# An FNet and GeGLU kernel: who issues two DRAM copies, and when one sum of x is formed

## The chip, the cores and the metric

The kernel runs on one core of a Trainium2 chip. A core has five engines with instruction queues of their own: TensorE (PE, with its weight loads shown as PEld), VectorE (DVE), ScalarE (ACT), GpSimd (POOL) and SyncE (SP). Sixteen DMA engines move the data for all of them. SP, ACT and POOL can each issue transfers; the profile counts those of SP as queue q1, those of ACT as q10 and those of POOL as q0. The metric is the device time in microseconds of one execution, as the median of several runs.

## What is computed

The input x has 2048 rows of 448 columns. Its rows are normalized to xn, and two results are formed from it:

```python
a = einsum("bsd,ed->bse", xn, dft_hid_re)        # 448 x 448
b = einsum("bsd,ed->bse", xn, dft_hid_im)
s = einsum("ts,bse->bte", dft_seq_re, a) - einsum("ts,bse->bte", dft_seq_im, b)   # 2048 x 2048
g = silu((gelu(xn @ w_gate) * (xn @ w_up)) @ w_down)      # 448 -> 1792 -> 448
out = x + s * g
```

Everything is float32. The kernel splits most operands into a rounded high part (the PE's fast 32-bit format) and the remainder, and multiplies high by high, high by low and low by high.

## The kernel before, in words

**The stages.** After a start of some 70 us (loads, norms, transposes, the first two feature blocks done plainly) comes the feed-forward stage: 24 *blocks*, two runs (p = 0 and 1) over features f = 2 to 13 in units of 128, each for half of the rows. Then comes the hidden transform (L988 and on), and then the long sequence transform with the matrices Cr and Ci (L1175 and on).

**One block** is the function `strassen` (L414). It forms gate and up projections of two row quarters with fewer products than the plain way: from sums of weights (s1 to s4) and sums of x (t1 to t4, and for the last columns tq). The order of the work on every engine is the order in which the Python code calls it (`manual_schedule`, L507). On PE, a block is five products x1 to x4 and x6 in five PSUM banks, with six matmuls of an earlier group's down projection (`down_one`, L372, reached by `send`) in four places of the block. The banks are the same in each block: x1 is bank 0, so the next block's first product x1 may not start before ScalarE has read this block's x1 for the gelu at L461.

On ScalarE, a block runs: a copy of x1 (L432), the high part of the late half's result (L499), the high part of the plain weights (L291), the high parts of the weight sums (L295, L296), in some blocks those of the down weights (L316) and of a sum of x (L711), the gelu of x1 (L461), the high part of the result (L477), and the second gelu (L493). VectorE subtracts the high parts and adds up the products; L299 and L300 are the low parts of the weight sums, L474, L475 and L490 handle the products.

**The weights' loop.** Each block prepares the next one's weights. SP loads the raw weights of the block after next as soon as the low parts are formed and the raw buffer is free (`load_s`, two transfers, L262 with 512 KB and L263 with 128 KB, issued behind L300). POOL forms the weight sums in the raw buffer (`sums_s`, L278 to L282) when both have landed. Then ScalarE (L295) and VectorE (L299, L300) split them, and the next load follows. So block b issues the load whose sums POOL forms in block b + 1, and which PE uses in block b + 2.

**Where the calls stand.** `strassen` gets three lists of steps: `preps[0]` runs behind x2, `preps[1]` behind the first half of x4, and `preps[2]` behind the gelu L461. It gets four steps `dn`, the down products, the last of which stands at the block's end, and two steps `late`, the unfinished end of the block before: `late[0]` stands behind x1 and `late[1]` behind x2.

**Sums in DRAM.** While these blocks run, the sums of Cr and Ci that the last stage needs are formed in DRAM, since only transfers are needed for it. For each pair j of output blocks (0 to 7), `sum_step` (L775) issues two copies of 896 KB each from the input `ca` to `sums[j]` (d = 0, in block n = 3j) and later two accumulating transfers of the same size onto them (d = 2, in block 3j + 2; for j = 0 one each in blocks 1 and 2). The copies are issued by SP (L788), ahead of the block's own steps, the accumulating ones by POOL (L790). As SP and POOL run ahead of PE, the copies of block 3j are issued right behind the weights' load of block 3j - 1, and the accumulating transfers of block 3j + 2 right behind POOL's weight sums in block 3j + 1. An accumulating transfer waits until its copy has landed.

**Sums of x for the second run.** Those are formed during the first run and in the first block of the second one, one step at a time. A step (`t_step`, L697) has three parts: the sum on VectorE (L701 to L706), its high part on ScalarE (L711), and its low part on VectorE (L715), which also issues the loads of the next step (`t_load`, L688: L691 and L695). The last two steps are `t1_steps[6]` and `t1_steps[7]`. In the first block of the second run (n = 12) the code at L897 to L901 puts the rest of step 6 into `preps`, the sum of step 7 into `preps[2]`, its high part into `dn[2]` and its low part into `dn[3]`. The first use of step 7 is in the next block, the third product (x3, L445).

Of the kernel before, what the change touches and what calls it, by code (L numbers as in the profile page):

```python
# [47 lines left out]
def fnet_geglu(ctx: ExitStack, tc: tile.TileContext, x, ca, ct, cp, et, wgu, wss, wd, out):  # L48
# [15 lines left out]
    nc = tc.nc  # L64
# [27 lines left out]
    def part(t, off, a, b):  # L92
        v = t[:, off : off + a * b].rearrange("p (a b) -> p a b", a=a)
        return v
# [209 lines left out]
    def load_d(grp):  # L304
        rv = a_r[:, 17 * P : 17 * P + 2 * D].rearrange("p (f d) -> p f d", f=2)
        nc.sync.dma_start(
            rv, wd[grp[0] * P : (grp[0] + 2) * P, :].rearrange("(f p) d -> p f d", p=P)
        )
        return rv
# [197 lines left out]
    with tc.manual_schedule():  # L507
# [180 lines left out]
        def t_load(i, p, k1, k2):  # L688
            c, e = 2 * p, 2 * p + 1
            for n, v in ({0: (e, k1), 1: (c, k1)}, {0: (e, k2)}, {1: (c, k2)}, {0: (e, k1)}, {})[i].items():  # L690
                nc.sync.dma_start(tmp(n), xw_at(*v))  # L691
            if i == 3:
                rows = [slice(0, P)] if k1 < 3 else [slice(0, 64), slice(64, P)]
                for r in rows:
                    nc.sync.dma_start(tmp(1)[r], xw_at(e, k2)[: r.stop - r.start])  # L695

        def t_step(i, places, p, k1, k2):  # L697

            a, b = tmp(0), tmp(1)

            def sub():  # L701
                if i == 1:
                    n = P if k1 < 3 else 64
                    nc.vector.tensor_sub(a[:n], a[:n], b[:n])
                else:
                    nc.vector.tensor_sub(b, *((a, b), None, (b, a), (b, a))[i])  # L706

            v = a if i == 1 else b

            def high():  # L710
                nc.scalar.activation(places()[T[i]][0], v, AF.Copy)  # L711

            def low():
                h, l = places()[T[i]]
                nc.vector.tensor_sub(l, v, h)  # L715
                t_load(i + 1, p, k1, k2)

            return sub, high, low
# [50 lines left out]
        late = (h1, l1)  # L769
# [5 lines left out]
        def sum_step(at):  # L775


            j, d = divmod(at, 3)
            halves = [slice(0, NS // 2), slice(NS // 2, NS)]
            if d == 1:  # L780
                halves = halves[:1] if j == 0 else []
            elif d == 2 and j == 0:
                halves = halves[1:]
            for n in halves if j < NK // 2 else []:
                a, b = sums[j][:, n], ca[j, min(d, 1), :, n]
                a, b = [v.rearrange("p k c -> p (k c)") for v in (a, b)]
                if d == 0:
                    nc.sync.dma_start(a, b)  # L788
                else:
                    nc.gpsimd.dma_start(a, b, accum_op=ALU.add)  # L790

# [14 lines left out]
        t1_steps = [t_step(i, t1_places, 1, 0, 1) for i in range(4)]  # L806
# [14 lines left out]
        def then(*steps):  # L821
            return lambda: [v() for v in steps]
# [7 lines left out]
        def weights(n):  # L830

            if n == len(blocks):
                return [], [], []
            slot = slots[2 if n == len(blocks) - 1 else n % 2]
            w_of[blocks[n]] = parts_of(slot)
            plain, high, low = split_s(slot)
            next_ = [lambda: load_s(blocks[n + 1][1])] if n + 1 < len(blocks) else []
            return [plain, lambda: sums_s(nc.gpsimd)], [high], [low, *next_]

        def weights_d(g):  # L840
            w_d[g], low_of[g] = prep_d(GROUPS[g], d_raw[0])
# [3 lines left out]
        def e_load(b):  # L845
            e_raw[b] = (a_r[:, : 2 * D], tmp01, tmp01, a_r[:, 2 * D : 4 * D])[b]
            nc.sync.dma_start(e_raw[b], et[b].rearrange("p r d -> p (r d)"))
# [3 lines left out]
        def e_split(b):  # L851

            r = e_raw[b]
            if b == 3:
                e_at[b] = []
                for i in range(2):
                    h, q = a_ws[:, 3584 + i * D :][:, :D], r[:, i * D : (i + 1) * D]
                    nc.scalar.activation(h, q, AF.Copy)
                    nc.vector.tensor_sub(h[64:], q[64:], h[64:].bitcast(F32))
                    e_at[b].append(h)  # L860
                return
            v = (a_ws[:, 1792:3584], a_d[1], a_ws[:, :1792])[b]
            split(v[:, : 2 * D], v[:, 2 * D :], r)
            e_at[b] = [v[:, i * D : (i + 1) * D] for i in range(4)]

        for n, (p, f) in enumerate(blocks):
            g = f // 2
            dn, q = [send] * 4, tq[p]
            prep = weights(n + 1)
            step = []  # L870
            if f % 2 == 0 and n:
                d_raw[0] = load_d(GROUPS[g])
            sum_step(n)
            if f % 2 and 1 < n < len(blocks) - 1 or n == len(blocks) - 2:
                prep[1].append(lambda: weights_d(g))
                prep[2].append(lambda: low_of[g]())
            if p == 0:
                if f == 2:
                    dn = [nop, send, nop, send]
                    nc.sync.dma_start(gsp[0], gacc[2].rearrange("p k d -> p (k d)"))  # L880
                elif f == 3:
                    dn = [nop, send, send, low_d]
                elif f == 4:

                    dn[0] = nop
                if 6 <= f < 12:
                    step = [t1_steps[f - 6]]
                elif f == 12:
                    step = [t1_steps[6][:1]]
                if f in (8, 11):  # L890

                    k = slice(0, 4, 3) if f == 8 else slice(1, 3)
                    for i in range(2):
                        v, w = [u[:, i * 2048 :][:, :2048] for u in (sp, a_x[1].bitcast(F32))]
                        v, w = [u.rearrange("p (k d) -> p k d", k=4)[:, k] for u in (v, w)]
                        nc.sync.dma_start(v, w)
            elif f == 2:  # L897
                q = None
                for v, w in zip(prep, (*t1_steps[6][1:], t1_steps[7][0])):
                    v.append(w)  # L900
                dn[2:] = [then(send, v) for v in t1_steps[7][1:]]  # L901
            elif f == 3:

                v = sb.tile([P, 8 * D], F32, name="gacc2", tag="u1")
                for c in range(2):
                    gacc[2 + c] = part(v, c * 4 * D, 4, D)
                    nc.sync.dma_start(v[:, c * 4 * D :][:, : 4 * D], gsp[c])
                v = sb.tile([P, 4096], FR, name="w2", tag="u0")
                slots.append((v[:, :WH], v[:, WH : WH + WL]))
            elif f == NF - 3:  # L910
                e_load(2)
            elif f == NF - 2:
                dn[1] = dn[3] = then(send, send)
                prep[2].append(lambda: e_split(2))
                prep[2].extend([lambda b=b: e_load(b) for b in (1, 0, 3)])
            elif f == NF - 1:
                prep[1].append(lambda: e_split(0))
                prep[2].extend([lambda: e_split(3), lambda: e_split(1)])
                dn = [then(send, send), send, nop, nop]
            if step:  # L920
                for v, w in zip(prep, step[0]):
                    v.append(w)
            prep = [then(*v) for v in prep]
            late = strassen(f, p, w_of[p, f], q, late, dn, prep)
            if p == 0 and f == 4:
                nc.sync.dma_start(gsp[1], gacc[3].rearrange("p k d -> p (k d)"))
            elif p == 0 and f == 5:
                t_load(0, 1, 0, 1)
            elif p == 0 and f == 9:
                t_load(0, 1, 3, 2)  # L930
            if f % 2:
                dq += [(g, c, w_d[g], kk) for c in (2 * p, 2 * p + 1) for kk in range(4)]
# [304 lines left out]
        for m, (j, k) in enumerate(units):  # L1237
# [4 lines left out]
            if k in KS:  # L1242
# [7 lines left out]
                for i in range(8):  # L1250
# [4 lines left out]
                    n = KX[(j + 1) % 2][i]  # L1255
                    a, b = [v.rearrange("p (b d) -> p b d", d=D) for v in (TS[n], td[n])]
                    a, b = a[:, PARTS[h]], b[:, PARTS[h]]
# [127 lines left out]
```

## Time and profile before

| what | value |
|---|---|
| median of 3 runs | 773.26 us (772.25 to 773.74) |
| profiled execution | 774.27 us, of which the span of the profile is 772.5 us |
| granted TensorE clock, mean | 0.998 |
| PE, DVE, ACT, POOL busy | 99%, 82%, 45%, 16% of the span |
| DMA | 162.05 MB, mean 210 GB/s |
| queue q1 (SP), q0 (POOL), q10 (ACT), share of 16 engines | 50.9%, 15.9%, 0.0% |
| the copies L788 | 16 on SP, first at 63.9 us, last at 356.3 us |
| the accumulating transfers L790 | 16 on POOL, first at 73.1 us, last at 375.7 us |

All times in rows of the trace are microseconds from the span's start. A timeline row gives the start, the duration, the engine, the line of the code, the operation, what it writes and reads, how many were merged, and in brackets how long the engine had been idle and what ended that. A row of a DMA on SP, ACT or POOL is the time of its issue; when it landed is shown by the view of one source line, as the time from issue to landing.

### The profile page before, as it was taken

How to read it: one execution, taken by the hardware profiler on the slowest of the kernel's cores; microseconds unless marked ns; L12 is line 12 of the kernel's file. 1: busy time of each engine (PE TensorE's matmuls, PEld its weight loads, DVE VectorE, ACT ScalarE, POOL GpSimd, SP SyncE). 2: the span in 40 equal slices, each digit the busy share in tenths (PEclk: the TensorE clock that was granted, in tenths of full speed). 3: DMA queues.
4: the chain of work that ended last, by engine and by line, in shares of the span. 5: the costliest groups of instructions: out<-in, count | busy, mean ns of one | idle time of the engine just before them, and what ended most of it. 6: DMA issues, size and time to landing. Idle time of an engine off the chain costs nothing.

```text
span 772.5 us, 11462 instructions
## 1 busy us (share of the span) xinstructions
PE 764.4 (99%) x4046; PEld 686.5 (89%) x4046; DVE 633.6 (82%) x1090; ACT 348.7 (45%) x490; POOL 120.9 (16%) x160
## 2 busy tenths in 40 slices
PE   8999999999999999999999999999999999999997
PEld 7988888888888888888889999999999999999896
DVE  7987779898988888888876677988878697969687
ACT  3766443443533343434344755544444444444341
POOL 2002232422413223223200000000000000000000
PEclk9999999999999999999999999999999999999999
DMA  8078666567658655464642732879796969797894
GB/s 296 15 207 256 139 214 162 179 207 192 228 137 292 157 185 131 170 159 167 153 181 84 316 141 75 273 243 304 224 344 190 344 193 353 207 312 225 283 287 164
DMA packets 80026, 162.05 MB, mean 210 GB/s; under 512 B 7904, under 2 KB 62560, under 8 KB 78432
## 3 DMA queue, kind: packets, MB, share of 16 engines
q1 hardware_dynamic: 74640, 134.79, 50.9%
q0 software_dynamic: 5184, 26.41, 15.9%
q8 instruction: 32, 0.52, 0.3%
q14 instruction: 26, 0.21, 0.1%
q10 hardware_dynamic: 144, 0.11, 0.0%
HBM read 139.13 MB, written 51.25 MB: 246 GB/s over the span
## 4 chain that ended last, share of the span: by engine, by line
PE 74%; DVE 11%; DMA 8%; issue 2%; ACT 2%; POOL 2%; SPq 0%; DVEq 0%; POOLq 0%
PE p L1182 17%; PE x L400 15%; PE po L378 12%; PE ab L998 9%; PE p L1185 8%; PE gu L327 3%; DMA raw<-wss 3%; PE x L412 3%; DMA ts_u<-td 2%; PE py L1202 1%; PE py L1204 1%; PE py L1203 1%; PE gu L545 1%; DMA raw<-sums 1%; DVE w L299 1%
## 5 line engine op out<-in xcount | busy, mean ns | idle before, releaser
L378 PE MATMUL po<-wd,hs 128*128 128x448 f32 x672 | 152.7, 366 | 0.0
L378 PEld LDWEIGHTS po<-wd,hs 128*128 128x128 f32 x672 | 125.8, 188 | 14.2
L400 PE MATMUL x<-xt,w 128*128 128x512 f32 x432 | 114.1, 391 | 0.0
L400 PEld LDWEIGHTS x<-xt,w 128*128 128x128 f32 x432 | 81.1, 188 | 15.3
L127 ACT ACTIVATE w<-raw 128x896 fp32r<-128x896 f32 (+1 forms) x59 | 53.6, 911 | 67.4 <-DVE raw L1088 47.6
L400 PE MATMUL x<-t,w 128*128 128x512 f32 x276 | 80.8, 391 | 0.0
L998 PE MATMUL ab<-w,xt 128*128 128x448 f32 x256 | 68.1, 365 | 0.0
L389 DVE TENSOR_TENSOR gacc<-gacc,po 128x448 f32<-128x448 f32 x96 | 58.5, 614 | 10.2 <-PE po L378 10.1
L400 PEld LDWEIGHTS x<-t,w 128*128 128x128 f32 x276 | 51.8, 188 | 9.3
L1227 POOL DMA_DIRECT2D cc<-x x14 | 12.3, 881 | 291.7 <-DVE raw L1087 102.9
L477 ACT ACTIVATE hs<-tmp 128x512 fp32r<-128x512 f32 x24 | 15.2, 633 | 94.4 <-DVE tmp L475 94.4
L1182 PE MATMUL p<-xt,w 128*128 128x448 f32 x168 | 54.3, 374 | 0.0
L278 POOL TENSOR_TENSOR raw<-raw 128x256 f32<-128x256 f32 x23 | 18.3, 796 | 213.3 <-DMA raw<-wss 179.5
L998 PEld LDWEIGHTS ab<-w,xt 128*128 128x128 f32 x256 | 48.1, 188 | 3.8
L127 ACT ACTIVATE w<-f 128x896 fp32r<-128x896 f32 (+1 forms) x34 | 30.2, 888 | 45.3 <-DVE f L1088 26.4
L128 DVE TENSOR_TENSOR w<-raw,w 128x896 fp32r<-128x896 f32 (+1 forms) x40 | 41.6, 1045 | 2.9 <-ACT w L127 2.5
L1087 DVE TENSOR_TENSOR raw<-raw 128x128 f32<-128x128 f32 x69 | 19.8, 287 | 22.4 <-DMA raw<-sums 22.4
L1182 PE MATMUL p<-ts_u,ts_tmp 128*128 128x448 f32 x112 | 37.2, 379 | 0.3 <-DVE cc L1216 0.3
L295 ACT ACTIVATE w<-raw 128x768 fp32r<-128x768 f32 x24 | 20.3, 844 | 38.1 <-POOL raw L282 38.1
L1182 PE MATMUL p<-ts_g,w 128*128 128x448 f32 x112 | 36.6, 375 | 0.0
L1182 PE MATMUL p<-hs,w 128*128 128x448 f32 x112 | 35.6, 374 | 0.0
L998 PE MATMUL ab<-wd,xt 128*128 128x448 f32 x96 | 35.1, 365 | 0.0
(274 smaller groups left out, 1841.4 us busy)
## 6 DMA issues: line engine op xcount, KB each, us to landing
sums<-ca SPq DMA_DIRECT2D x16, 896.0 KB, 8.7
sums<-ca POOLq DMA_DIRECT2D x16, 896.0 KB, 9.6
raw<-ct SPq DMA_DIRECT2D x69, 192.0 KB, 4.1
raw<-wss SPq DMA_DIRECT2D x24, 512.0 KB, 3.9
ts_u<-td SPq DMA_DIRECT2D x24, 448.0 KB, 6.5
ts_g<-td SPq DMA_DIRECT2D x24, 448.0 KB, 6.2
raw<-sums SPq DMA_DIRECT2D x69, 128.0 KB, 4.2
f<-ct SPq DMA_DIRECT2D x39, 192.0 KB, 3.9
```

Source lines behind the costliest of these rows:

```text
L127: nc.scalar.activation(h, src, AF.Copy)
L128: nc.vector.tensor_sub(l, src, h)
L295: nc.scalar.activation(h[:, :n], src[:, :n], AF.Copy)
L327: nc.tensor.matmul(ps[:, cols], a, xt[:, k, cols], start=n == 0, stop=n == len(mm) - 1)
L378: nc.tensor.matmul(po[:, :D], hs[:, a, kk * P : (kk + 1) * P], wdn[:, b, i], start=n == 0, stop=n == 5,)
L389: nc.vector.tensor_add(ga, ga, po[:, :D])
L400: nc.tensor.matmul(ps, a[i], b[j], start=first and n == 0, stop=n == 2, skip_group_check=True)
L412: nc.tensor.matmul(ps, a[0], x_, start=False, stop=True, skip_group_check=True)
L998: nc.tensor.matmul(p[:, :D], a, b, start=n == 0, stop=n == len(mm) - 1)
L1087: nc.vector.tensor_add(s2, cr1, s1)
L1182: nc.tensor.matmul(ps[q][:, :D], h, v, start=u % UN == 0, stop=False, skip_group_check=True)
L1185: nc.tensor.matmul(ps[q][:, :HD], l, v[:, :HD], start=False, stop=u % UN == NS - 1, skip_group_check=True,)
```

## The change

SP no longer issues the copies. In blocks 3j they become a step of `preps[2]`: ScalarE issues them behind the gelu L461. As the step is appended after the weights' own steps, the copies stand behind `low` and `load_s` of that block in the code, but in another queue. The accumulating transfers stay where they were.

In block n = 12, the sum and the high part of the last step of x both move to the end of the block (`dn[3]`), and the low part moves into the next block, behind `late[0]`.

```diff
                 if d == 0:
-                    nc.sync.dma_start(a, b)
+                    nc.scalar.dma_start(a, b)
                 else:
                     nc.gpsimd.dma_start(a, b, accum_op=ALU.add)
...
-            sum_step(n)
+            if n % 3:
+                sum_step(n)
+            else:
+                prep[2].append(lambda: sum_step(n))
...
             elif f == 2:
                 q = None
-                for v, w in zip(prep, (*t1_steps[6][1:], t1_steps[7][0])):
+                for v, w in zip(prep, t1_steps[6][1:]):
                     v.append(w)
-                dn[2:] = [then(send, v) for v in t1_steps[7][1:]]
+                dn[3] = then(send, *t1_steps[7][:2])
             elif f == 3:
 
+                late = then(late[0], t1_steps[7][2]), late[1]
                 v = sb.tile([P, 8 * D], F32, name="gacc2", tag="u1")
```

No instruction is added or taken away on PE, DVE or POOL. ScalarE gains 16 DMA issues and SP loses them. The second part changes the place of one sum, one high part and one low part.

## The prediction

> **What bounds the kernel now.** I read the page's first part, then the waits, those of PE alone first, then the timeline of single engines.
>
> ```profile
> PE 764.4 (99%) x4046; PEld 686.5 (89%) x4046; DVE 633.6 (82%) x1090; ACT 348.7 (45%) x490; POOL 120.9 (16%) x160
> ```
> ```profile
> PE x L412 <- DVE xt L715: 0.5, 1, 0.5
> PE p L1182 <- DVE cc L1216: 0.3, 1, 0.3
> ```
> ```profile
> 175.98 0.86 PE L400 MATMUL x<-xt,w 128*128 128x512 f32 x3
> 189.75 0.86 PE L400 MATMUL x<-xt,w 128*128 128x512 f32 x3
> ```
>
> PE is busy all the time. Behind the start, the longest wait that it has is 0.5 us, once, for the low part of the last sum of x. The two timeline rows are the first products of blocks 8 and 9: a block takes 13.77 us, and PE works through all of it. So the change can win that 0.5 us and nothing else in the feed-forward stage. What it can lose is the reserve that now keeps the other engines ahead of PE. These waits show where they wait:
>
> ```profile
> POOL raw L278 <- DMA raw<-wss: 179.5, 19, 14.2
> ACT hs L477 <- DVE tmp L475: 94.4, 24, 6.7
> ACT w L295 <- POOL raw L282: 38.1, 18, 3.7
> ```
>
> POOL waits for the weights' load in 19 blocks, and ScalarE waits for POOL's sums in 18. ScalarE works in order, and the gelu L461 stands behind L295. The next block's first product overwrites the bank that L461 reads. So a late load becomes a late L282, a late L295, a late L461, and in the end a wait of PE. The question is how much reserve that chain has, and what the copies in their new place take of it.
>
> **One cycle as it is (j = 2, blocks 6 to 8).** The rows are from the timelines of ScalarE, SP, POOL and PE, and from the views of the two transfers' source lines.
>
> ```profile
> 157.25 0.58 ACT L461 ACTIVATE tmp<-x 128x512 f32<-128x512 f32 x1
> 160.60 0.43 SPq L263 DMA_DIRECT2D raw<-wss  x1
> DMA to landing us min/median/max: 3.6/3.6/3.6
> ```
> ```profile
> 164.32 0.74 POOL L278 TENSOR_TENSOR raw<-raw 128x256 f32<-128x256 f32 x1 [10.06 <-DVE tmp L490]
> 168.33 1.67 POOL L790 DMA_DIRECT2D sums<-ca  x2
> ```
> ```profile
> L790 POOL DMA_DIRECT2D sums<-ca x2: 803/962/1122, 168.3 to 168.9; - x2
> ...
> DMA to landing us min/median/max: 7.8/10.2/12.7
> ```
> ```profile
> L263 SPq DMA_DIRECT2D raw<-wss x1: 384/384/384, 173.7 to 173.7; - x1
> ...
> DMA to landing us min/median/max: 8.5/8.5/8.5
> ```
> ```profile
> 182.33 0.74 POOL L278 TENSOR_TENSOR raw<-raw 128x256 f32<-128x256 f32 x1 [12.33 <-DMA raw<-wss]
> 186.49 0.85 ACT L295 ACTIVATE w<-raw 128x768 fp32r<-128x768 f32 x1 [3.71 <-POOL raw L282]
> 188.07 0.58 ACT L461 ACTIVATE tmp<-x 128x512 f32<-128x512 f32 x1
> ```
>
> Block 6 issues its load at 160.60, nothing else is in flight, and it lands in 3.6 us. POOL starts its sums at 164.32 and, 4.0 us later (168.33), the two accumulating transfers, which land by 168.9 + 12.7 = 181.6. The load of block 7, issued at 173.67 beside them, lands at 173.67 + 8.5 = 182.2: it took 8.5 us in place of 3.6 and came 0.6 us behind the older transfer of another queue. POOL starts at 182.33, ScalarE at 186.49, and L461 ends at 188.65. PE's block 9 begins at 189.75. The reserve of this cycle is 1.1 us.
>
> **The change part by part. Copies from ScalarE.** Today they are issued behind the load of the block before, in the same queue, so they never stand ahead of a load that anyone waits for soon. In the new place ScalarE issues them when L461 ends (157.83 in block 6), and SP issues the second part of the same block's load 2.8 us later (160.60). Now the 1.8 MB are ahead, in another queue.
>
> How late does that load land? No row shows ScalarE's queue beside SP's, so I bound X, the time from the end of L461 to the landing of the load. If the copies do not hold it at all, it is 164.2 - 157.83 = 6.4 us. The other end is the time for both amounts together:
>
> ```profile
> 273.27 0.34 SPq L262 DMA_DIRECT2D raw<-wss  x1
> ```
> ```profile
> L788 SPq DMA_DIRECT2D sums<-ca x2: 526/561/596, 274.1 to 274.7; - x2
> ...
> DMA to landing us min/median/max: 6.9/7.7/8.4
> ```
>
> Here one load (its first part at 273.27) and two copies went one behind the other, and the last copy landed at 274.7 + 8.4 = 283.1: 9.9 us for all. X lies between 6.4 and 9.9. I take 8.6, nearer to the upper end, because the nearest row, the load beside the accumulating transfers, shows it landing last.
>
> From X the cycle follows. POOL needs 4.1 us from the landing to the accumulating transfers (164.2 to 168.33), so these come at 157.83 + X + 4.1, later than today by d = X - 6.4. The load of block 7 ends with them, as it does today, so L461 of block 8 is late by d, and PE waits d less the reserve of 1.1 us: 8.6 - 6.4 - 1.1 = 1.1 us. This cycle occurs for j = 1 to 6; the rows of the first and the last of the six are
>
> ```profile
> 115.60 0.58 ACT L461 ACTIVATE tmp<-x 128x512 f32<-128x512 f32 x1
> 126.24 1.66 POOL L790 DMA_DIRECT2D sums<-ca  x2
> 146.21 0.58 ACT L461 ACTIVATE tmp<-x 128x512 f32<-128x512 f32 x1
> 148.43 0.86 PE L400 MATMUL x<-xt,w 128*128 128x512 f32 x3
> ```
> ```profile
> 322.56 0.60 ACT L461 ACTIVATE tmp<-x 128x512 f32<-128x512 f32 x1 [0.80 <-PE x L400]
> 353.37 0.58 ACT L461 ACTIVATE tmp<-x 128x512 f32<-128x512 f32 x1
> 356.25 0.86 PE L400 MATMUL x<-xt,w 128*128 128x512 f32 x3
> ```
>
> For j = 1 the new time of the accumulating transfers is 116.18 + 8.6 + 4.1 = 128.9, so d = 2.6, and the reserve is 148.43 - 146.79 = 1.6: PE waits 1.0 us. For j = 6 the reserve is 356.25 - 353.95 = 2.3 and d is 1.7: no wait. Worked the same way, the six are 1.0, 1.1, 1.5, 0, 1.7 and 0, together **5.3 us**. At X = 6.4 the six are 0; at 9.9 they are 12.5.
>
> The copies of j = 7 meet no weights' load behind their accumulating transfers, and cost nothing. Those of j = 0 are issued in block 0, while in the old place SP issues them some 15 us earlier:
>
> ```profile
> 73.10 0.85 POOL L790 DMA_DIRECT2D sums<-ca  x1
> 78.36 0.60 ACT L461 ACTIVATE tmp<-x 128x512 f32<-128x512 f32 x1 [2.05 <-PE x L400]
> 85.24 0.74 POOL L278 TENSOR_TENSOR raw<-raw 128x256 f32<-128x256 f32 x1 [11.29 <-DMA raw<-wss]
> ```
>
> The first accumulating transfer (73.10) now has to wait for a copy issued at 78.96, which by the 6.9 to 8.4 us above lands at 86 to 87; POOL's next sums (85.24) stand behind it and start 2 to 3 us late. The gelu of that block and the next block's first product have these rows:
>
> ```profile
> 90.35 0.58 ACT L461 ACTIVATE tmp<-x 128x512 f32<-128x512 f32 x1
> 93.21 2.22 PE L400 MATMUL x<-xt,w 128*128 128x512 f32 x9
> ```
>
> Six of the nine matmuls end the block and three begin the next, so that one begins near 94.6, and the gelu, which ends at 90.93, has 3.6 us in hand. I cost this at nothing, at most 1 us.
>
> ScalarE pays for the issue of two transfers, 0.5 to 0.6 us each on SP (the row of L788 above: 526 to 596 ns). Behind them stands L477, and ScalarE idles before it anyway, 94.4 us in 24 blocks, or 3.9 us each. That idle time hides the 1.1 us; without it L477 would come 1.1 us late in eight blocks, and it is a down product of a later block that reads it. SP is rid of 16 issues, and nothing waited for them.
>
> **The last sum of x.**
>
> ```profile
> 244.25 0.69 DVE L706 TENSOR_TENSOR tmp<-tmp 128x512 f32<-128x512 f32 x1 [1.49 <-DMA tmp<-xw]
> 249.62 0.93 DVE L715 TENSOR_TENSOR xt<-tmp,xt 128x512 fp32r<-128x512 f32 x1
> 250.60 0.50 PE L412 MATMUL x<-xt,w 128*128 128x512 f32 x1 [0.48 <-DVE xt L715]
> ```
>
> VectorE now waits 1.49 us for a load at 242.8, is late from there on, and PE waits 0.48 us for the low part. With the sum at the block's end, L474 and what follows move 1.4 us up, but sum, high part and low part now stand one behind the other, 0.69 to 0.93 us each, and the low part comes behind the late half's product (L497). I estimate its end near 250.3, against 250.55 now, and PE needs it at 250.1. The gain lies between 0 and 0.5; I take 0.3.
>
> **The sum.** 5.3 - 0.3 = +5.0 us on the profiled execution: 774.3 + 5.0 = 779.3 us. That execution (774.27, of which 772.5 are the span) lies 1.0 us above the median of the runs, 773.26; so I predict a median of **778.3 us**.
>
> **A rule beside it.** In the Trainium skill, DMA: Bandwidth & Descriptors says in "Issuing engines are not separate DMA queues" that transfers of all issuing engines run on the same 16 DMA engines and interleave, so that another issuer saves only the time of the issue. The load that came 0.6 us behind POOL's transfers agrees, and it speaks against the change. The same page says in "Queues, rings and completion order" that each DMA engine takes turns between queues, a packet at a time. By that rule the load could pass between the two copies, which is the first rival here.
>
> **The rivals.** First, not slower: the load gets its turn behind the first copy. One copy and one load then land by the time that one load and the first copy take above, 6.9 us. With X = 6.9 the waits are 0 in every cycle, and the gain of 0.3 is all that is left: 774.0, a median of **773.0 us**. It decides at X = 7.4 or so, below which only the cycles j = 2, 3 and 5 lose a few tenths. For it speaks that the load is a third of the copies' size; against it, that beside POOL's transfers the load got no such turn.
>
> Second, the full hold: X = 9.9, since the slowest DMA engine lands last. Then the sum is 12.5 - 0.3, or 786.5, a median of **785.5 us**. Against it speaks that it needs the load's last part behind the last copy on every engine.
>
> Third, the second edit does not do what it says: the low part is still the last to come, and PE waits as long as before. That costs the 0.3 us and changes neither sign nor case.
>
> **How the numbers follow.** The forecast (X from about 7.8 to 9.4, a median of 775 to 782.5) has 0.52; no hold, 0.36; the full hold, 0.10; a gain that I do not see, beyond the 0.5 us, 0.02. A measurement of this kernel can tell about 0.2%, or 1.5 us, from no change. No hold lies within it; forecast and full hold are slower. That gives slower 0.62, same 0.36, faster 0.02. The range runs from 772.6 (no hold with the whole 0.5 us) to 783.5: it takes in no hold and the forecast and leaves out most of the full hold.
>
> **What would show it.** In the profile after, queue q10 carries the copies, about 14 MB, and q1 as much less. Right if: the load L263 of blocks 3, 6, 9 and so on lands 5.5 us or more after its issue; POOL's L790 comes 1 to 4 us later in its block; and PE's waits list x1 (L400, or L412) behind ScalarE's L461, some 1 to 2 us each in three or four blocks, 5 us in all. Wrong if that load still lands in under 5 us: then PE shows no such wait, and the first rival holds. If the load is late but PE does not wait, the reserve was larger than I read it. For the second edit: L706 without a wait for its load, and PE's wait for L715 gone or shorter.

## The result, and the profile after

The changed kernel takes **786.2 us** (median of 4 runs, 785.0 to 787.2); the kernel before took 772.75 us on the same chip (4 runs). The ratio is 1.0173, with a 95% interval of 1.0155 to 1.0191: 13.5 us slower. The forecast was 778.3 us with a range up to 783.5, so the sign was right and the loss was more than twice the one forecast. The profiled execution took 787.11 us, of which the span is 785.3 us, 12.8 us more than before.

The page of the changed kernel, the busy times of its first part, and the line by engine of the chain that ended last:

```profile
PE 768.0 (98%) x4046; PEld 686.8 (87%) x4046; DVE 631.6 (80%) x1090; ACT 348.0 (44%) x490; POOL 120.6 (15%) x160
```
```profile
PE 63%; DMA 16%; DVE 8%; POOL 6%; ACT 3%; issue 2%; SPq 1%; ACTq 0%; DVEq 0%; POOLq 0%
```

The same line of the kernel before:

```profile
PE 74%; DVE 11%; DMA 8%; issue 2%; ACT 2%; POOL 2%; SPq 0%; DVEq 0%; POOLq 0%
```

The instructions on PE are the same, though they are busy 3.6 us longer (768.0 against 764.4). In the chain, 8 points more now run over transfers, and 4 over POOL. PE's own waits in the changed kernel (group, total us, times, longest) show where PE meets them:

```profile
PE x L400 <- DVE tmp L454: 6.4, 3, 2.7
PE x L400 <- ACT tmp L461: 2.7, 3, 1.2
```

Before, the longest of the feed-forward stage was 0.5 us. Now there are 9 us in six places, those for L461 that the prediction had named, and larger ones for L454 that it had not. And the waits along the weights' loop, to be held against 179.5 and 38.1 us before:

```profile
POOL raw L278 <- DMA raw<-wss: 193.6, 20, 13.3
```
```profile
ACT w L295 <- POOL raw L282: 61.8, 20, 5.1
```

The cycle that the prediction followed (j = 2, blocks 6 to 8), from the timelines of ScalarE, SP, POOL and PE and the view of one source line:

```profile
162.53 0.50 ACTq L788 DMA_DIRECT2D sums<-ca  x1
...
162.98 0.58 ACT L461 ACTIVATE tmp<-x 128x512 f32<-128x512 f32 x1
163.07 0.61 ACTq L788 DMA_DIRECT2D sums<-ca  x1
```
```profile
166.33 0.43 SPq L263 DMA_DIRECT2D raw<-wss  x1
179.92 0.39 SPq L263 DMA_DIRECT2D raw<-wss  x1
```
```profile
L788 ACTq DMA_DIRECT2D sums<-ca x2: 497/554/610, 162.5 to 163.1; - x2
...
DMA to landing us min/median/max: 5.4/6.5/7.6
```
```profile
172.75 0.74 POOL L278 TENSOR_TENSOR raw<-raw 128x256 f32<-128x256 f32 x1 [12.76 <-DMA raw<-wss]
176.82 1.67 POOL L790 DMA_DIRECT2D sums<-ca  x2
190.52 1.33 POOL L278 TENSOR_TENSOR raw<-raw 128x256 f32<-128x256 f32 x1 [12.03 <-DMA raw<-wss]
```
```profile
194.64 0.84 ACT L295 ACTIVATE w<-raw 128x768 fp32r<-128x768 f32 x1 [4.24 <-POOL raw L282]
196.22 0.58 ACT L461 ACTIVATE tmp<-x 128x512 f32<-128x512 f32 x1
```
```profile
152.91 0.86 PE L400 MATMUL x<-xt,w 128*128 128x512 f32 x3
...
197.25 0.86 PE L400 MATMUL x<-xt,w 128*128 128x512 f32 x3
```

Every link of the predicted chain is there. The load of block 6, issued at 166.33, reaches POOL's sums at 172.75, 6.4 us later in place of 3.7. It comes 2 us behind the last copy (163.07 + 7.6 = 170.6). The accumulating transfers follow at 176.82, the next load (179.92) reaches POOL only 10.6 us later in place of 8.7, L461 of block 8 ends at 196.80, and PE begins block 9 at 197.25. From block 6 to block 9 PE needs 44.34 us, where it needed 41.32.

### The profile page after: what moved, and what is told of

Its sections match the earlier page's. It is cut to its first block, busy times and chain, and to the rows that moved or that the text cites. A ratio compares the mean times of both kernels' runs of the same rounds, so it can differ in the third digit from the quotient of the medians.

```text
span 785.3 us, 11463 instructions
## 1 busy us (share of the span) xinstructions
PE 768.0 (98%) x4046; PEld 686.8 (87%) x4046; DVE 631.6 (80%) x1090; ACT 348.0 (44%) x490; POOL 120.6 (15%) x160
## 4 chain that ended last, share of the span: by engine, by line
PE 63%; DMA 16%; DVE 8%; POOL 6%; ACT 3%; issue 2%; SPq 1%; ACTq 0%; DVEq 0%; POOLq 0%
PE p L1186 21%; DMA raw<-wss 12%; PE p L1189 10%; PE ab L1002 9%; PE po L378 7%; PE x L400 6%; PE gu L327 3%; DMA tmp<-xw 2%; DVE w L299 2%; POOL raw L279 2%; PE py L1206 1%; PE py L1208 1%; PE py L1207 1%; POOL raw L278 1%; DVE w L300 1%
## 5 line engine op out<-in xcount | busy, mean ns | idle before, releaser
L378 PEld LDWEIGHTS po<-wd,hs 128*128 128x128 f32 x672 | 126.2, 189 | 14.4
L400 PE MATMUL x<-xt,w 128*128 128x512 f32 x432 | 116.7, 398 | 9.4 <-DVE tmp L454 6.4
L278 POOL TENSOR_TENSOR raw<-raw 128x256 f32<-128x256 f32 x23 | 20.4, 887 | 221.5 <-DMA raw<-wss 193.6
L295 ACT ACTIVATE w<-raw 128x768 fp32r<-128x768 f32 x24 | 20.3, 845 | 61.8 <-POOL raw L282 61.8
L292 DVE TENSOR_TENSOR w<-raw,w 128x640 fp32r<-128x640 f32 x24 | 22.0, 915 | 23.2 <-ACT w L291 23.1
```

Source lines behind the costliest of these rows:

```text
L278: eng.tensor_add(r[:, 1:16:14], r[:, 0:14:13], r[:, 9:17:7])
L292: nc.vector.tensor_sub(l[:, n:], src[:, n:WL], h[:, n:WL])
L295: nc.scalar.activation(h[:, :n], src[:, :n], AF.Copy)
L378: nc.tensor.matmul(po[:, :D], hs[:, a, kk * P : (kk + 1) * P], wdn[:, b, i], start=n == 0, stop=n == 5,)
L400: nc.tensor.matmul(ps, a[i], b[j], start=first and n == 0, stop=n == 2, skip_group_check=True)
```

## The experiments

Each kernel was run beside the kernel before; the ratios are to that kernel's runs on the same chip (medians of 771.6 to 772.5 us). The chips differ from one group of kernels to the next. So where two changed kernels are compared, the difference of their medians stands first, and what the two ratios give, on 772.5 us, in brackets.

**One part of the change at a time.** Copies alone:

```diff
-                for v, w in zip(prep, t1_steps[6][1:]):
+                for v, w in zip(prep, (*t1_steps[6][1:], t1_steps[7][0])):
                     v.append(w)
-                dn[3] = then(send, *t1_steps[7][:2])
+                dn[2:] = [then(send, v) for v in t1_steps[7][1:]]
...
-                late = then(late[0], t1_steps[7][2]), late[1]
```

> The first part of the change alone: ScalarE issues the copies behind the gelu L461; the last sum of x stays where the kernel before has it. Theory (the place of the copies, ahead of the same block's load): all of the loss, 786 us, 785 to 788, with PE's waits for L454 and L461 as in the changed kernel. Rival (the moved sum of x carries part of it): clearly under 785.

Measured: 793.5 us, ratio 1.0277 (1.0256 to 1.0298), 7.3 us *slower* than the whole change (8.0), where theory and rival had 786 or less. The moved sum is no part of the loss; it takes some of it away. The timelines of VectorE and PE show where:

```profile
262.34 0.69 DVE L706 TENSOR_TENSOR tmp<-tmp 128x512 f32<-128x512 f32 x1 [6.10 <-DMA tmp<-xw]
```
```profile
265.07 0.96 PE L400 MATMUL x<-t,w 128*128 128x512 f32 x3 [2.88 <-DVE tmp L479]
...
268.39 0.80 PE L412 MATMUL x<-xt,w 128*128 128x512 f32 x1 [2.12 <-DVE xt L715]
```

The copies of j = 4 are issued in block 12 and hold the load of the last sum's operand too. VectorE stands 6.1 us in front of L706, with L474 and the rest of the block behind it, and PE waits twice, in block 13. That block takes 21.8 us of PE here (258.30 to 280.11), against 14.9 in the changed kernel and 14.5 before: 5.0 us are these two waits, and besides, the granted clock is 0.84 over the block, where it is 1.00 in the other two. At the block's end, where the change puts it, L706 waits 1.2 us and nothing urgent is behind it.

The last sum alone (copies on SP in their old place):

```diff
-                    nc.scalar.dma_start(a, b)
+                    nc.sync.dma_start(a, b)
...
-            if n % 3:
-                sum_step(n)
-            else:
-                prep[2].append(lambda: sum_step(n))
+            sum_step(n)
```

> The second part of the change alone: the last sum of x at the block's end, the copies issued by SP in their old place. Theory: 772.4 us, 0 to 0.5 under the kernel before, PE's wait for L715 0.2 us in place of 0.5. Rival (the moved sum costs time): over 774.

Measured: 772.5 against 771.6 us, ratio 1.0005 (0.9992 to 1.0018). PE's wait for L715 is gone from its list, but the 0.5 us cannot be seen in the time. By itself the second part is worth nothing.

**Place against queue.** The copies issued by SP, behind the load:

```diff
-                    nc.scalar.dma_start(a, b)
+                    nc.sync.dma_start(a, b)
```

> The changed kernel, but SP issues the copies, in the same place of the code (behind the block's load). In one queue they then stand behind the load, 0.9 us after it, and cannot hold it. Theory (the order of copies and load): 772 to 774 us, load L263 landing in 4 us. The copies come some 13 us later than in the kernel before, so the accumulating transfers may wait for them up to 3 us, which could give back 1 or 2 us. Rival (what counts is that the copies run in this part of the block, beside the load, in whatever order): 780 us or more.

Measured: 782.0 us, ratio 1.0130 (1.0109 to 1.0152). My theory missed here by 8 us, and the rival's number came. The load is indeed free: issued at 166.74, it lands in 3.6 us. But the copies are late for the two things that come after them (waits, VectorE's timeline, and the landing of L695, the load of an operand of x behind the copies in the queue, issued at 169.04):

```profile
POOL sums L790 <- DMA sums<-ca: 30.3, 12, 15.7
```
```profile
179.37 0.69 DVE L706 TENSOR_TENSOR tmp<-tmp 128x512 f32<-128x512 f32 x1 [4.22 <-DMA tmp<-xw]
```
```profile
DMA to landing us min/median/max: 9.9/9.9/9.9
```

POOL waits for copies 12 times, with its next sums behind. The operand of x lands 9.9 us after its issue, and L706 holds L446 and L454 for 4.2 us. So it is not only the weights' load that the copies must stay clear of.

The copies on ScalarE, at the head of the block:

```diff
-            if n % 3:
-                sum_step(n)
-            else:
-                prep[2].append(lambda: sum_step(n))
+            sum_step(n)
```

> The changed kernel, but with the copies at the head of the block in the code: ScalarE issues them in front of L432, some 8 us ahead of the same block's load in place of 3. They are still ScalarE's, in its own queue. Theory (the load falls into the copies' 7 to 8 us): most of the loss is gone, 772.5 to 774, load L263 landing in 4 to 5 us. Rival (ScalarE's issue time or the second queue as such): 784 us or more, as in the changed kernel.

Measured: 773.4 us, ratio 1.0023 (1.0008 to 1.0038). Of the 13.5 us all but 1.8 are back, with the same issuer and the same queue. In block 6 the copies leave at 151.15 and 151.69, and the load of 160.25 lands in 5.1 us. It is the place that costs, not ScalarE's issue time nor its queue.

**Where the loss becomes a wait.** Without the accumulating transfers:

```diff
-                else:
+                elif j == 0:
                     nc.gpsimd.dma_start(a, b, accum_op=ALU.add)
```

> The changed kernel without the accumulating transfers of j = 1 to 7 (the sums of Cr and Ci stay copies, so the last stage computes with other matrices; j = 0 is as it was). The copies still hold the same block's load. Theory (the held load costs only because the accumulating transfers come late and hold the next load until PE's reserve is gone): 772 to 776 us, load L263 behind the copies still 6 to 7 us, the next one under 5. Rival (the held load and the x loads behind it make PE wait directly): 781 us or more.

Measured: 773.1 us, ratio 1.0017 (1.0000 to 1.0034), although the load beside the copies still takes 6.0 us in block 6; the next one takes 3.6. All that is left of PE's waits in the feed-forward stage is

```profile
PE x L412 <- DVE xt L715: 0.2, 1, 0.2
```

So the late load alone costs nothing that can be measured; the loss needs the accumulating transfers behind it. That it is their lateness which costs, and not that they run at all, is read from the timelines: this kernel leaves 14 of them out altogether.

The steps ahead of L454 moved behind it:

```diff
-            return [plain, lambda: sums_s(nc.gpsimd)], [high], [low, *next_]
+            return [lambda: sums_s(nc.gpsimd)], [plain, high], [low, *next_]
...
-                for v, w in zip(prep, step[0]):
+                for v, w in zip(prep[1:], step[0]):
                     v.append(w)
+                if len(step[0]) > 2:
+                    dn[3] = then(dn[3], step[0][2])
```

> The changed kernel with the steps that stand ahead of L446 and L454 moved behind them: the high and low part of the plain weights (L291, L292) and the sum of x. The changed kernel's trace shows 6.4 us of PE waits for L454, 2.7 for L461. Theory A (the path of the prediction, L282 to L295 to L461, ends last in every cycle, and the waits for L454 only stand in front of it): 783 to 787 us, PE's waits now for L461, in sum about 8. Theory B (the path L291, L292, sum of x, L454, which the prediction did not follow, carries the loss): 779 us or less.

The high parts of the weight sums behind L461:

```diff
-            return [plain, lambda: sums_s(nc.gpsimd)], [high], [low, *next_]
+            return [plain, lambda: sums_s(nc.gpsimd)], [], [high, low, *next_]
```

> The changed kernel with the high parts of the weight sums (L295, L296) behind the gelu L461 in place of ahead of it, so that L461 no longer stands behind POOL's sums. Theory A (L461 ends last in every cycle, L454 within half a us of it in three): the 2.7 us of waits for L461 go, those for L454 stay: 781 to 785 us. Theory B (L454 alone carries the loss): 785 us or more.

Both (the last line then is `return [lambda: sums_s(nc.gpsimd)], [plain], [high, low, *next_]`):

> Both moves together, with the copies where the change puts them. Theory (PE is held by these two paths and by nothing else): 773 to 776 us, no wait of PE over 0.5 us in the feed-forward stage, although load L263 still lands 6 to 7 us after its issue and the accumulating transfers stay late. Rival (the load itself is late for PE's use, or the DMA engines are the bound): 780 us or more.

The sum of x alone (the second part of the first of these diffs):

> The changed kernel with one move alone: the sum of x, which waits for its loads behind the weights' load in SP's queue, stands behind L454 in place of ahead of it; L291 and L292 stay. Theory (the sum of x waits last, 1.2 us in block 5, and takes 0.8 itself; L292 is the one before it): about half of the 6.8 us that both moves brought, 781 to 784 us. If the sum of x alone makes L454 late: 779.5; if L292 alone: 786.

And a control, the kernel before with the moves of the first:

> A control: the kernel before with the two moves (L291, L292 and the sum of x behind L454), the copies in their old place. Theory: 771 to 773.5 us, no difference, since PE waits for none of them there; then what the moves brought to the changed kernel is the removed wait. If the moves bring or cost something by themselves, it shows here.

| kernel | us | ratio (95%) |
|---|---|---|
| L454 freed | 779.4 | 1.0105 (1.0090 to 1.0120) |
| L461 freed | 786.4 | 1.0210 (1.0171 to 1.0249) |
| both | 780.1 | 1.0107 (1.0089 to 1.0124) |
| sum of x alone | 783.9 | 1.0146 (1.0127 to 1.0165) |
| control | 772.2 | 1.0000 (0.9986 to 1.0013) |

PE's longest waits of the first three in the feed-forward stage, in this order:

```profile
PE x L400 <- ACT tmp L461: 4.3, 4, 1.5
```
```profile
PE x L400 <- DVE tmp L454: 5.5, 2, 3.6
```
```profile
PE x L412 <- DVE w L300: 1.8, 3, 1.1
...
PE x L400 <- DVE tmp L490: 1.3, 1, 1.3
```

Freeing L454 takes off 6.8 us (5.3), of which the sum of x alone takes off 2.3 (2.1), and PE then waits for L461 as predicted, 4.3 us in place of 2.7. Freeing L461 takes off nothing: PE waits for L454 as before. (The profiled execution of that kernel took 792.6 us, with a granted clock of 0.50 from 192.9 to 199.7 us; its median is 786.4.) This move also puts L295, and with it the low parts and the next load, behind the gelu; what that costs by itself was not run. Theory A, by which the waits for L454 only stand in front of L461, missed both numbers, and expected 8 us of waits for L461; theory B had 786.4 and missed 779.4 by 0.4 us. With both freed PE waits for L300, the low part of the weights themselves, and for L490 once, and the time is no better than with L454 alone. That misses my 773 to 776; the rival, with the load late for PE's own use, had it. So L454 is the dearer of the two, but no single consumer is *the* cause: the weights arrive late, and each way by which they reach PE is late in its turn. The control shows that the moves which free L454 bring nothing where nothing is late; the move that frees L461 has no such control.

**What is carried from j = 0.**

```diff
-                    nc.scalar.dma_start(a, b)
+                    (nc.scalar if j else nc.sync).dma_start(a, b)
...
-            if n % 3:
+            if n % 3 or n == 0:
                 sum_step(n)
```

> The changed kernel, but the two copies of j = 0 are issued by SP at the head of block 0, as in the kernel before. The prediction had costed their move at 0 to 1 us; in the changed kernel's trace L461 of block 3 ends 2.9 us later than before, with PE only 0.2 later. Theory (that lateness is carried by the weights' loop into the cycle of j = 1 and is paid there): 782.5 to 784.5 us, block 3's L461 ends near 116.2 and the accumulating transfers of j = 1 come near 128.3 in place of 131.2. Rival (each cycle starts with its own reserve): 786 us, as the changed kernel.

Measured: 783.9 us, ratio 1.0154 (1.0132 to 1.0176), 2.3 us less than the changed kernel (1.5; the two intervals overlap). L461 of block 3 and the first product of block 6 (where PE waits now for L461):

```profile
115.98 0.57 ACT L461 ACTIVATE tmp<-x 128x512 f32<-128x512 f32 x1
```
```profile
150.61 0.97 PE L400 MATMUL x<-xt,w 128*128 128x512 f32 x3 [0.99 <-ACT tmp L461]
```

The gelu is back at its old time, and block 6 begins 2.3 us earlier than in the changed kernel. The accumulating transfers of j = 1 come at 129.84, half-way between the theory's 128.3 and the changed kernel's 131.2. So in the traces the two copies of j = 0, at the start of the stage, cost 2.3 us by block 6; the whole time supports it, but not clear of its noise.

**Half the amount.** One copy of each pair on SP at the block's head, one on ScalarE behind the gelu:

```diff
-                    nc.scalar.dma_start(a, b)
+                    (nc.scalar if n.start else nc.sync).dma_start(a, b)
...
-                prep[2].append(lambda: sum_step(n))
+                sum_step(n, slice(0, 1))
+                prep[2].append(lambda: sum_step(n, slice(1, 2)))
```

> The changed kernel with one of the two copies of each j issued by SP at the block's head, and only the other by ScalarE behind the gelu. Theory (the same block's load lands behind what ScalarE has put ahead of it; the first of the two copies lands 5.4 us after its issue, about when an unhindered load does): load L263 lands in 4 to 5 us, 773 to 777 us. Rival (any transfer ahead of the load holds it in full): 782 us or more.

Measured: 772.2 us, ratio 0.9992 (0.9978 to 1.0005). With 896 KB ahead of it the load of block 6 lands in 5.1 us, and over the whole stage PE has one wait of more than 0.2 us:

```profile
PE x L400 <- DVE tmp L454: 1.2, 1, 1.2
```

The loss does not grow in proportion: half the amount costs nothing, the whole 13.5 us. That is what a reserve does.

**Both uncounted causes out.** The diffs of the freed L454 and of j = 0 together:

> The changed kernel with both causes taken out that the prediction had not counted: the copies of j = 0 in their old place, and L291, L292 and the sum of x behind L454. What is left is the path that the prediction priced. Theory (the causes add): 786.2 less 6.8 less 2.3, or 777.1 us, that is 4.6 over the kernel before, where the prediction had 5.0. Rival (they overlap, or the prediction's own terms were wrong too): 779 us or more, or 775 or less.

Measured: 780.5 us, ratio 1.0104 (1.0077 to 1.0131). The causes do not add; this is no better than the freed L454 alone. In the profiled execution, at 777.1 us the lowest of the six, PE waits 2.7 us for L461 and none for L454, and the six cycles together lose 5.2 us, the size of my forecast. That is luck in part: cycle by cycle they lose 0.0, 1.1, 2.0, 1.4, 0.6 and 0.1, where the forecast had 1.0, 1.1, 1.5, 0, 1.7 and 0. By the median, what is left is 8 us, not 5; in which cycles the longer executions lose the rest was not seen.

No version beat the kernel before by more than can be measured.

## Why the prediction was wrong in size

**What bounds the kernel, and what it could win: right.** The second part of the change alone moves nothing that can be measured.

**The landing of the load (X, the main estimate): right in its number, in part by luck.** X was taken as 8.6 us, between 6.4 and 9.9. In the six cycles it was 7.9, 9.1, 8.7, 10.1, 8.5 and 8.8, a mean of 8.85. The first of the six loads, from the view of the source line:

```profile
L263 SPq DMA_DIRECT2D raw<-wss x1: 427/427/427, 119.9 to 119.9; - x1
...
DMA to landing us min/median/max: 7.1/7.1/7.1
```

The prediction let ScalarE issue the copies when L461 ends. They left 1.0 to 2.4 us before that (162.53 against 163.56 in block 6), and counted from the first copy's issue the load landed after 10.1 to 11.7 us, in every cycle later than the 9.9 that the prediction took as the longest. The two errors largely cancelled.

The first rival (the load gets its turn behind the first copy, X = 6.9) fell: no load did better than 7.9. Its 6.9 was misread besides: it is the first copy's own time, and from the load's issue it is 274.14 + 6.9 - 273.27 = 7.8, which by the prediction's sum gives some 775 us and not 773.0. The Trainium skill, DMA: Bandwidth & Descriptors, "Queues, rings and completion order", has each DMA engine take turns between queues packet by packet. The load of block 6, which landed 2.0 us behind the last copy of another queue, does not show such sharing at this scale. Its first part was issued at 165.94; the DMA view from 166 to 169 us (packets, MB, share of 16 engines) has the copies' queue q10 and, with one packet, SP's q1:

```profile
q10 hardware_dynamic: 168, 1.08, 101.9%
q1 hardware_dynamic: 1, 0.00, 0.3%
```

In the same 3 us of the load of block 5 (issued at 152.11), which has no copies ahead, q1 moved 239 packets.

**L461 as what PE meets last: half right.** In all six cycles PE begins the block 0.05 to 0.45 us after L461 has ended. But where PE waited for L454 first, freeing L461 gained nothing: the two paths are late together.

**Each cycle priced with its own reserve: wrong, and the largest miss.** The prediction put the gelu of the copies' block at its old time in every cycle and took the reserve off anew. The rows for j = 1 and j = 6 after, from PE's and ScalarE's timelines, show otherwise:

```profile
107.34 0.87 PE L400 MATMUL x<-xt,w 128*128 128x512 f32 x3
```
```profile
118.53 0.58 ACT L461 ACTIVATE tmp<-x 128x512 f32<-128x512 f32 x1
...
151.95 0.58 ACT L461 ACTIVATE tmp<-x 128x512 f32<-128x512 f32 x1
```
```profile
328.65 0.97 PE L400 MATMUL x<-xt,w 128*128 128x512 f32 x3 [1.16 <-ACT tmp L461]
...
370.74 0.98 PE L400 MATMUL x<-xt,w 128*128 128x512 f32 x3 [0.36 <-ACT tmp L461]
```
```profile
337.77 0.57 ACT L461 ACTIVATE tmp<-x 128x512 f32<-128x512 f32 x1
```

and PE before, for the same two blocks:

```profile
107.11 0.86 PE L400 MATMUL x<-xt,w 128*128 128x512 f32 x3
```
```profile
314.93 0.86 PE L400 MATMUL x<-xt,w 128*128 128x512 f32 x3
```

In block 3 L461 ended 116.18 - 107.11 = 9.07 us behind PE's start of the block; now it ends 119.11 - 107.34 = 11.77 behind it, 2.7 us later, before the copies of j = 1 have moved anything (those of j = 0 have). In block 18 it was 8.23 and is 9.69. Where PE has just waited for L461, the reserve is gone, and the next copies start from there. The cycles, in us:

| j | X | L461 later against PE | old reserve | loss forecast | loss measured |
|---|---|---|---|---|---|
| 1 | 7.9 | 2.7 | 1.6 | 1.0 | 4.2 |
| 2 | 9.1 | 1.2 | 1.1 | 1.1 | 3.0 |
| 3 | 8.7 | 1.2 | 1.6 | 1.5 | 3.1 |
| 4 | 10.1 | 1.4 | 1.3 | 0 | 1.3 |
| 5 | 8.5 | 0.2 | 2.5 | 1.7 | 1.9 |
| 6 | 8.8 | 1.5 | 2.3 | 0 | 0.8 |

Loss measured is the time from PE's start of block 3j to that of block 3j + 3, after less before; for j = 1, (152.91 - 107.34) - (148.43 - 107.11) = 4.25. The six make 14.3 us against 5.3, and the third column, which the prediction had at nothing, adds up to 8.2, against the 9.0 that are missing. With the measured X the prediction's own formula gives 6.6 us; with the third column added to d as well it gives 3.0, 2.8, 2.8, 2.9, 1.8 and 1.1, or 14.4. So some 7.8 us are lateness carried into a cycle, and 1.3 the landing of the load. The sum agrees better than its terms: j = 1 comes out 1.3 us too low and j = 4 1.6 too high. By block 21 PE is 14.5 us late (370.74 against 356.25), at the end of the span 12.8; the stages behind it gave 1.7 back, and why stays open. The weights' loop could have been read as a whole from before: the three loads of a cycle took 3.7 + 8.7 + 3.4 us until POOL began, and the way from POOL's begin to the next load took 7.1 in block 8 (182.33 to 189.46), 37.1 in all, against 41.3 for three blocks of PE:

```profile
189.46 0.43 SPq L263 DMA_DIRECT2D raw<-wss  x1
```
```profile
192.90 0.74 POOL L278 TENSOR_TENSOR raw<-raw 128x256 f32<-128x256 f32 x1 [6.45 <-DMA raw<-wss]
```

After the change the loads take 6.4 + 10.6 + 3.6 (the last from 197.99 to 201.55), and the same sum is 41.9. By this sum the loop has no slack left against PE's 41.3, so nothing is regained between cycles. In other blocks the way took 6.7 (223.32 to 230.03 in block 11, before); with 6.7 the sum is 40.7, and 0.6 us could be regained in a cycle. That this is why the lateness persists is argued from these sums, not shown by a run of its own; and the sum isn't the whole price: the three blocks took 44.3, and the half amount (5.2 + 10.3 + 3.6 and three times 7.1, or 40.4) lost 1.5 us in this cycle, though its median shows no loss.

**The copies of j = 0, costed at 0 to 1 us: wrong.** POOL waited 11.1 us for the first of them, the loop was 2.9 us late at L461 of block 3, and j = 1 paid: 2.3 us by the traces of the experiment, 1.5 to 2.3 by its times.

**The path by L291, L292, the sum of x and L454: not seen.** It stands on the same late load, without POOL's sums in between:

```profile
144.49 0.83 DVE L292 TENSOR_TENSOR w<-raw,w 128x640 fp32r<-128x640 f32 x1 [3.23 <-ACT w L291]
146.51 0.77 DVE L704 TENSOR_TENSOR tmp<-tmp 128x512 f32<-128x512 f32 x1 [1.19 <-DMA tmp<-xw]
...
147.98 0.69 DVE L454 TENSOR_TENSOR tmp<-tmp,x 128x512 f32<-128x512 f32 x1
```

VectorE is held twice here (3.2 and 1.2 us) by work that PE does not need yet, ahead of L454, which PE does need. Putting that work behind took off 6.8 us. How these divide between L454 itself and the loop, which also ran some tenths faster at each step, stays open: in the changed kernel L461 ended no more than 0.45 us before PE began, so L454 alone could not have cost that.

**The gain of the second part, 0 to 0.5 us: right alone, wrong beside the first.** Together with the copies it saves 7.3 us (8.0), since the load that L706 waits for is one more transfer behind them. I priced the two parts apart.

**The second rival** (785.5 us) came nearest to the time, and the packets bear out its picture of the load behind both copies. But it let the copies leave when L461 ends, so it needed X = 9.9 in every cycle, and it too priced each cycle with its own reserve.

## What to carry to other kernels

Before a transfer is moved, list all that is loaded behind it, in every queue, until it has landed (here the held load landed 10.1 to 11.7 us after the first copy had been issued), and each instruction that waits for one of these with urgent work behind it on its engine. Price lateness round the whole loop that feeds the busy engine, not cycle by cycle: add up the loop's shortest time and hold it against the period as a first bound, since a reserve that was used once isn't there in the next cycle. And free a consumer only when the supply itself is on time; otherwise the next consumer waits in its place.

## What was not expected of the hardware

ScalarE's queue issues a transfer ahead of activations that precede it in the code and have not begun. In block 3 the copies left 1.8 us before the gelu that they were put behind began, and 0.1 us after L295, the last activation in front of them that had to wait:

```profile
116.63 0.85 ACT L295 ACTIVATE w<-raw 128x768 fp32r<-128x768 f32 x1 [2.39 <-POOL raw L282]
116.73 1.15 ACTq L788 DMA_DIRECT2D sums<-ca  x2
...
118.53 0.58 ACT L461 ACTIVATE tmp<-x 128x512 f32<-128x512 f32 x1
```

In block 6 the first copy left 0.1 us after L711, which had waited there, had begun (162.44). So a transfer's place behind an instruction in an engine's code does not make it leave after that instruction has run.

Behind a wait, PE can run at a lower granted clock for a while. After the 2.45 us in block 5, six matmuls took 2.93 us that took 1.66 behind the shorter wait of block 11. In the view by windows the granted clock (the first number behind POOL's, as a share of full speed) is 0.57 for these 4 us, and 1.00 in the 4 us on either side:

```profile
148.72 2.93 PE L400 MATMUL x<-xt,w 128*128 128x512 f32 x6 [2.45 <-DVE tmp L454]
```
```profile
148.00:152.00 4.00, 3.28 (x8) 2.65 (x9) 2.76 (x4) 2.47 (x5) 1.42 (x3) 0.57 0.00 0
```

The Trainium skill, TensorE: Matmul & The Clock Gate, "Part 1: The HAM clock gate", has the clock halved after an idle window of some 3.4 us. Here an idle of 2.45 us was enough, while one of 2.71 us (block 8, at 194.53) was followed by a granted clock of 1.00 from 194 to 198 us. And the drop can come later: with SP's copies behind the load, PE began again at 181.51 after 3.26 us, the first six matmuls took 1.73 us, and only then the granted clock fell to 0.50:

```profile
183.00:186.40 3.40, 3.40 (x10) 2.91 (x9) 3.26 (x5) 0.00 (x0) 0.00 (x0) 0.50 0.99 205
```

In the changed kernel the drop in block 5 cost no more than 0.4 us: the next block could not begin before L461 of block 5 had ended, at 152.53, and it began at 152.91.
